# One half of an attention block issued a unit earlier, its scales with it, and some weight conversions and one small transpose issued later

## The chip, the cores and the metric

The kernel runs on one core of one Trainium2 chip. The metric is the device time of one execution in microseconds (us). Five engines work side by side, each through its own list of instructions in a fixed order, and wait for each other through semaphores: PE (TensorE, matrix products into PSUM), DVE (VectorE), ACT (ScalarE), POOL (GpSimd) and SP (SyncE, which here only issues transfers).

## The reference

Attention inside chunks of 64 rows, for 8 batches and 8 heads of 576 rows and 64 columns, and then a feed-forward layer over the 4608 tokens of 512 numbers that this gives:

```python
scores = scale * np.matmul(q_c, k_c.transpose(0, 1, 2, 4, 3))
scores = scores - np.max(scores, axis=-1, keepdims=True)
attn = np.exp(scores)
attn = attn / (np.sum(attn, axis=-1, keepdims=True) + 1e-09)
out = np.matmul(attn, v_c)
...
h = x @ w_in            # 4608 x 512 times 512 x 2048
g = h - np.tanh(h)
return (g @ w_out)      # 4608 x 2048 times 2048 x 512
```

## The kernel before

The tokens are taken in nine groups of 512. Group 0 and group 1 get their attention in a first phase, and their feed-forward layer in full precision (class `FeedForward`). Groups 2 to 8 run with fp16 pairs and a way of multiplying 2x2 blocks with seven products instead of eight (class `Fast`). So two things have to be made ready while group 1 is under way: the fp16 weights, and the attention of group 2. While group g of the seven runs, the attention of group g+1 is made.

**Units.** Group 1 runs in 16 units, called W0 to W15 here (`written`, line 540). A unit makes a first product (line 511, 12 matmuls of 512 columns, into one of two `ph` buffers in PSUM), `shrink` (tanh on ACT at line 518, a subtraction on DVE at line 520, both in place of `ph`), and the second product of an older unit (line 538). What DVE rounds off for the unit before, line 528, ends the use of that unit's `ph`: so the first product of W10 waits for line 528 of W8. Groups 2 to 8 run in 16 units each, F0 to F15 for group 2 (`run`, line 661): a first product (line 590, 24 matmuls), tanh (line 597), `L598` on DVE (the last reader of `ph`), three operations on POOL (lines 599 to 601), and one unit later `split` (line 610 on ACT and 611 on DVE). The second product (line 630, 21 matmuls) uses a unit that is two or three units old. F0 to F3 have no second product of their own, F4 has two, and from F5 each has one.

**What is put between.** The dictionary `at` holds more work by half-units: key 2s is issued behind the first product and `shrink` of unit s, key 2s+1 behind its second product, and keys from 32 on belong to group 2 (32 is F0). An engine meets this work at that place of its list and nowhere else. Three kinds of work lie there:

- the attention of the next group, put by `ahead` (line 695), in two halves b = 0 and 1. First for both: absolute sums of q and k (line 105, ACT), the largest of v (line 288, DVE); `across` turns these sums with a small transpose on PE (line 296) and takes their maximum on DVE (line 298); `spread_out` hands it to all partitions by two tiny matmuls (line 305) and makes the scales `to` (lines 112 to 114, DVE). Then per half: `split` of q, k and v to fp16 pairs with these scales (line 322 on ACT, 323 on DVE), scores (line 333, 96 matmuls on PE), shift (345, 346), exponent (350), totals (355 to 358), division (362), a transpose by DMA (369, 370, 374), and values (333 again, 386, 387). All PSUM work of this kind has one buffer, `psa`.
- `convert` of the first weight matrix (lines 432, 433, 435 and 436), one of 16 in each unit.
- `combine` of the second weight matrix, eight times (lines 450 to 463, POOL), and behind it `shorten` in four parts to fp16 (line 480 on ACT, 481 on DVE). A combination also waits until the one that used its place was shortened.

The order of all engines in this stage is the order in which the program is written (`manual_schedule`).

Of the kernel before, what the change touches and what calls it, by code (L numbers as in the profile page):

```python
# [38 lines left out]
FAST = 2  # L39
# [16 lines left out]
def attn_ffn_kernel(ctx: ExitStack, tc: tile.TileContext, qE, kE, vE, qL, kL, vL, w_in, w_out, out):  # L56
# [41 lines left out]
    def new_half_x():  # L98

        t = xpool.tile([P, KC, MOST], F32R, name="xh").bitcast(F16)  # L100
        return t[:, :, :MOST], t[:, :, MOST:]
# [593 lines left out]
    def ahead(att, at, g):  # L695

        o = 2 * FC * (g - FAST)

        def put(unit, part, f, *args):
            at[o + 2 * unit + part].append(lambda: f(*args))  # L700

        late = g == FAST
        for unit, n in (1, "q"), (2, "k"):
            put(unit, 0, lambda n=n: att.sums(g, n, ffn.tile([P, MOST], F32, name="t", bufs=3)))
        put(1 if g < FAST + 2 else -3, 0, att.halves, g, 0)
        put(1 if late else 2, 1, att.halves, g, 1)
        put(3 if late else 4, 1, att.across, g)
        put(4 if late else 5, 1, att.spread_out, g)
        put(9, 1, lambda: powers.update({g: half.power_of(g)}))
        put(6, 0, lambda: xs.update({g: new_half_x()}))  # L710
        for b, u in enumerate((4, 13) if late else (6, 14)):
            put(u, 1, att.split, g, b, "q")
            put(u + 1, 0, att.split, g, b, "k")
            other = u + 2 if late and b else u + 1
            put(other, 1, att.split, g, b, "v")
            if g + 1 < NG:
                for i in (2 * b, 2 * b + 1):
                    put(u + 1, 1, att.load, FIRST[g + 1] + i, i, "qk")
                    put(other, 1, att.load, FIRST[g + 1] + i, i, "v")
            u += late  # L720
            put(u + 2, 0, att.scores, g, b)
            put(u + 2, 1, att.shifted, g, b)
            put(u + 3, 0, att.exponent, g, b)
            put(u + 3, 1, att.totals, g, b)
            put(u + 4, 0, att.divided, g, b)
            put(u + 5, 0, att.transpose, g, b)
            at[o + 2 * u + 17 - late].insert(0, lambda b=b: att.values(g, b, xs[g]))
# [15 lines left out]
    att = Early(pool, [psum, ps_a], 4)  # L743
# [102 lines left out]
    late = ctx.enter_context(tc.tile_pool(name="att", bufs=1, side="right", reuse_waits="tile"))  # L846
    w_pool.update((fc, late) for fc in SPARE)
    att, half = Late(late), Half(late)
# [4 lines left out]
    xs, powers, at, made = {}, {}, defaultdict(list), {}  # L853
    def make(j, steps):
        if j not in made:
            made[j] = half.combine(j)
        for _ in range(steps):
            next(made[j])
# [11 lines left out]
    for g in range(FAST, NG):  # L870
        ahead(att, at, g)
    for j in range(FC // 2 - 2):
        at[4 * j + 7].append(lambda j=j: make(j, 5 if j else 4))
        if j == 0:
            at[11].append(lambda: make(0, 1))
        for i in range(4):
            at[4 * j + 11 + i].append(lambda j=j, i=i: half.shorten(j, slice(i, i + 1)))
    o = 2 * FC
    for k, j, steps in (o - 1, 6, 5), (o + 1, 7, 2), (o + 3, 7, 1), (o + 5, 7, 1), (o + 7, 7, 1):
        at[k].append(lambda j=j, steps=steps: make(j, steps))  # L880
# [77 lines left out]
```

## Time and profile before

| | |
|---|---|
| median of 3 runs | 812.99 us (812.72 to 813.47) |
| the profiled execution's own time | 813.85 us |
| its span, first to last instruction | 812.0 us |
| mean granted TensorE clock | 1.000 |
| F0 begins on PE at | 217.52 us |
| idle PE before a line-511 product, waiting for line 528 on DVE | 5 times, 4.0 us in all (this counts the weight loads in front of the products) |
| POOL waiting for line 598 | 223.3 us in 102 waits |

All views are of the profiled execution. A row of the timeline has the start in us, the duration in us, the engine, the line, the operation with its output and inputs, the count of merged instructions, and, in brackets, how long the engine had been idle and what ended the wait. A row of the chain has start, share of time on the chain, and what the time went to; durations on the chain leave out what overlaps.

### The profile page before, as it was taken

The page shows a single profiled execution, that of the slowest core. Times are in us where ns is not written, and L with a number is a line of the kernel's source. Part 1 is how long each engine was busy: PE and PEld are TensorE (multiplying, and loading weights), DVE is VectorE, ACT ScalarE, POOL GpSimd, SP SyncE. Part 2 cuts the span into 40 slices and gives each one's busy share as a digit, 9 for nine tenths or more (in the row PEclk, how much of TensorE's full clock was granted, in tenths as well). Part 3 has the DMA queues.
Part 4 walks back from the last instruction along what each step waited for, and adds up shares of the span by engine and source line. Part 5 has one row for each costly group of instructions (what it writes and reads, how often), then busy time and mean ns, then how long its engine had stood idle before and what let it go on. Part 6 is the DMA issues. An engine that isn't in the chain of part 4 may idle for free.

```text
span 812.0 us, 21336 instructions
## 1 busy us (share of the span) xinstructions
PE 798.3 (98%) x9141; PEld 680.7 (84%) x9141; DVE 644.8 (79%) x866; ACT 469.1 (58%) x748; POOL 420.6 (52%) x463
## 2 busy tenths in 40 slices
PE   8999999999999999999999999999999999999997
PEld 4677787777778888888888888888888888888886
DVE  6899997799998968696869687868786878777553
ACT  5698768656776546454745474536454555454332
POOL 1100002296586656574656566565656665656563
PEclk9999999999999999999999999999999999999999
DMA  6954524102221313122222222222222220202000
GB/s 250 343 186 158 170 95 151 63 17 27 66 79 31 96 34 95 38 79 46 80 48 80 53 80 54 79 54 79 53 80 53 80 52 3 54 2 53 2 27 27
DMA packets 59038, 63.23 MB, mean 78 GB/s; under 512 B 32832, under 2 KB 40000, under 8 KB 58944
## 3 DMA queue, kind: packets, MB, share of 16 engines
q1 hardware_dynamic: 58512, 61.23, 25.4%
q8 instruction: 71, 1.16, 0.6%
q10 hardware_dynamic: 432, 0.66, 0.2%
q14 instruction: 23, 0.19, 0.1%
HBM read 45.09 MB, written 9.44 MB: 67 GB/s over the span
## 4 chain that ended last, share of the span: by engine, by line
PE 81%; DVE 9%; ACT 7%; issue 2%; POOL 0%; DVEq 0%; ACTq 0%
PE ph L590 35%; PE po L630 31%; PE ph L511 6%; PE po L538 5%; PE psa L333 3%; PE ph L777 1%; ACT w L131 1%; ACT wh L140 1%; ACT junk L108 1%; ACT s L213 1%; DVE wl L481 1%; DVE gl L528 1%; DVE w L136 1%; ACT gh L527 1%; DVE wl L435 1%
## 5 line engine op out<-in xcount | busy, mean ns | idle before, releaser
L590 PE MATMUL ph<-xh,wl 128*128 128x256 f16 x2520 | 291.3, 273 | 0.3 <-DVE xl L598 0.3
L590 PEld LDWEIGHTS <-wl 128*128 128x128 f16 x2520 | 244.8, 98 | 29.9 <-issue 1.0
L599 POOL TENSOR_TENSOR xl<-xl 128x256 f32<-128x256 f32 x112 | 110.2, 984 | 224.0 <-DVE xl L598 223.3
L597 ACT ACTIVATE t<-ph,sig 128x512 f32<-128x512 f32 x112 | 77.0, 687 | 195.1 <-PE ph L590 193.5
L598 DVE SCALAR_TENSOR_TENSOR xl<-ph,sig,t 128x512 f32<-128x512 f32 x112 | 83.6, 746 | 75.4 <-ACT t L597 75.0
L630 PEld LDWEIGHTS <-wh 128*128 128x128 f16 x1176 | 114.9, 98 | 13.4
L601 POOL TENSOR_TENSOR xl<-xl 128x256 f32<-128x256 f32 x112 | 112.5, 1004 | 0.0
L600 POOL TENSOR_TENSOR xl<-xl 128x128 f32<-128x128 f32 x112 | 107.1, 956 | 0.0
L630 PE MATMUL po<-wl,wh 128*128 128x256 f16 x672 | 104.7, 273 | 0.0
L611 DVE SCALAR_TENSOR_TENSOR gl<-xl,to_g,gh 128x896 f16<-128x896 f32 x56 | 85.4, 1525 | 9.8 <-ACT gh L610 9.6
L630 PE MATMUL po<-wh,wh 128*128 128x256 f16 x504 | 88.6, 273 | 0.0
L611 DVE SCALAR_TENSOR_TENSOR wh<-xl,to_g,wh 128x896 f16<-128x896 f32 x56 | 66.6, 1189 | 27.4 <-ACT wh L610 27.4
L610 ACT ACTIVATE wh<-xl,to_g 128x896 f16<-128x896 f32 x56 | 58.2, 1039 | 49.5 <-POOL xl L601 49.5
L630 PEld LDWEIGHTS <-gh 128*128 128x128 f16 x784 | 75.7, 98 | 9.2
L630 PE MATMUL po<-wh,gh 128*128 128x256 f16 x392 | 63.5, 273 | 0.0
L630 PE MATMUL po<-wl,gh 128*128 128x256 f16 x392 | 61.1, 273 | 0.0
L610 ACT ACTIVATE gh<-xl,to_g 128x896 f16<-128x896 f32 x56 | 57.8, 1032 | 1.2 <-POOL xl L601 1.2
L538 PE MATMUL po<-wh,gh 128*128 128x512 f32 x128 | 52.1, 407 | 0.9 <-ACT gh L527 0.5
L538 PE MATMUL po<-wl,gh 128*128 128x512 f32 x128 | 50.7, 396 | 0.9 <-POOL wl L144 0.9
L410 POOL PARTITION_ALL_REDUCE top<-most x2 | 0.7, 371 | 97.7 <-DVE most L408 97.7
L630 PEld LDWEIGHTS <-gl 128*128 128x128 f16 x392 | 38.3, 98 | 4.5
L630 PE MATMUL po<-wh,gl 128*128 128x256 f16 x196 | 40.5, 273 | 0.0
(147 smaller groups left out, 1352.9 us busy)
## 6 DMA issues: line engine op xcount, KB each, us to landing
raw<-w_in SPq DMA_DIRECT2D x16, 512.0 KB, 3.6
raw<-w_out SPq DMA_DIRECT2D x16, 512.0 KB, 4.5
rawk<-kL SPq DMA_DIRECT2D x28, 256.0 KB, 3.3
rawv<-vL SPq DMA_DIRECT2D x28, 256.0 KB, 3.6
xl<-qL SPq DMA_DIRECT2D x28, 256.0 KB, 3.2
out<-wh SPq DMA_DIRECT2D x55, 128.0 KB, 1.8
q<-qE SPq DMA_DIRECT2D x8, 256.0 KB, 5.4
v<-vE SPq DMA_DIRECT2D x8, 256.0 KB, 5.0
```

Of the source, the lines that this page charges most:

```text
L333: nc.tensor.matmul(ps(c, e, hp)[u * D:(u + 1) * D], lhsT=stationary(a, r, e, hp, u), rhs=moving(b, r, e, hp, u), start=(i == 0), stop=(i = ...
L511: nc.tensor.matmul(ph, lhsT=wt[fc][0][a][:, kc * P:(kc + 1) * P], rhs=x[b][:, kc, cols], start=(k == 0), stop=(k == 3 * KC - 1))
L538: nc.tensor.matmul(self.po[t], lhsT=gg[a][:, ts], rhs=wt[fc][1][b], start=(fc == 0 and a == b), stop=(fc == FC - 1 and a == 1))
L590: nc.tensor.matmul(self.ph[:, 1 - f::2, :], lhsT=half_w[fc][:, w, kc * P:(kc + 1) * P], rhs=rhs, start=(k == 0), stop=(k == 3 * KC - 1))
L597: nc.scalar.activation(t, self.ph, AF.Tanh, scale=sig)
L598: nc.vector.scalar_tensor_tensor(out=u[:, :4], in0=self.ph, scalar=sig, in1=t, op0=ALU.mult, op1=ALU.subtract)
L599: nc.gpsimd.tensor_add(u[:, 4:6], u[:, 1:3], u[:, 0:4:3])
L600: nc.gpsimd.tensor_add(u[:, 6], u[:, 1], u[:, 2])
L601: nc.gpsimd.tensor_sub(u[:, 0:4:3], u[:, 0:2], u[:, 2:4])
L610: nc.scalar.activation(gh, u, AF.Copy, scale=powers[1])
L611: nc.vector.scalar_tensor_tensor(out=gl, in0=u, scalar=powers[1], in1=gh, op0=ALU.mult, op1=ALU.subtract)
L630: nc.tensor.matmul(place[m], lhsT=part[:, self.SUM[m]], rhs=w[m][:, o], start=first, stop=(last and part is gl), skip_group_check=True)
```

## The change

```diff
@@ ahead(): the attention of group g, issued while the group before runs
-        put(3 if late else 4, 1, att.across, g)
-        put(4 if late else 5, 1, att.spread_out, g)
+        later = g == FAST + 1
+        put(2 if late else 4 + later, not later, att.across, g)
+        put(3 if late else 5, not late, att.spread_out, g)
         put(9, 1, lambda: powers.update({g: half.power_of(g)}))
         put(6, 0, lambda: xs.update({g: new_half_x()}))
-        for b, u in enumerate((4, 13) if late else (6, 14)):
+        for b, u in enumerate((3, 13) if late else (6, 14)):
@@ conversions of the combined weights
         for i in range(4):
-            at[4 * j + 11 + i].append(lambda j=j, i=i: half.shorten(j, slice(i, i + 1)))
+            at[4 * j + 11 + i + (2 if j > 3 and i else 0)].append(lambda j=j, i=i: half.shorten(j, slice(i, i + 1)))
```

`late` is true for group 2 alone, whose attention runs under W0 to W15. Its `across` moves from behind the second product of W3 to behind that of W2, its `spread_out` from behind the second product of W4 to behind the first product of W3, and every step of its half 0 moves one unit ahead, with the loads of the next group that follow it. For group 3 (the fourth) `across` moves from behind the second products of F4 to behind the first product of F5; its `spread_out` stays behind the second product of F5. For the combinations j = 4 and 5 (the fifth and sixth), the parts 1 to 3 of `shorten` move one unit back. No instruction is added or taken out.

Three places show it. The first is DVE's list around F3 to F6. The names: `xl<-ph` (line 598) belongs to F4 and F5 in turn, line 611 to F3 and F4, line 298 is the maximum in `across` of group 3, and lines 112 to 114 are its `spread_out`. Before:

```order
L481 SCALAR_TENSOR_TENSOR wh_2619<-wl_2611,to_w,wh_2619 128x512
L598 SCALAR_TENSOR_TENSOR xl<-ph,sig,t 128x512
L611 SCALAR_TENSOR_TENSOR wh_2633<-xl,to_g,wh_2632 128x896
L481 SCALAR_TENSOR_TENSOR wl_2620<-wh_2612,to_w,wl_2620 128x512
L298 TENSOR_REDUCE most<-psa 3x1
L598 SCALAR_TENSOR_TENSOR xl<-ph,sig,t 128x512
L611 SCALAR_TENSOR_TENSOR gl<-xl,to_g,gh 128x896
L481 SCALAR_TENSOR_TENSOR wh_2621<-wh_2608,to_w,wh_2621 128x256
L112 TENSOR_SCALAR from<-psa 128x3
```

The same place of the changed kernel (buffer numbers differ by two):

```order
L481 SCALAR_TENSOR_TENSOR wh_2617<-wl_2609,to_w,wh_2617 128x512
L598 SCALAR_TENSOR_TENSOR xl<-ph,sig,t 128x512
L611 SCALAR_TENSOR_TENSOR wh_2631<-xl,to_g,wh_2630 128x896
L481 SCALAR_TENSOR_TENSOR wl_2618<-wh_2610,to_w,wl_2618 128x512
L598 SCALAR_TENSOR_TENSOR xl<-ph,sig,t 128x512
L611 SCALAR_TENSOR_TENSOR gl<-xl,to_g,gh 128x896
L298 TENSOR_REDUCE most<-psa 3x1
L481 SCALAR_TENSOR_TENSOR wh_2619<-wh_2606,to_w,wh_2619 128x256
L112 TENSOR_SCALAR from<-psa 128x3
```

Line 298 now stands behind line 598 of F5 and line 611 of F4; on PE, line 305 still stands behind the second product of F5, and the first product of F6 behind line 305.

The second place is ACT's list from F1 to F2. Line 480 is `shorten`, line 562 writes out group 1's result, the two rows of line 597 are tanh of F1 and F2. Before:

```order
L597 ACTIVATE t<-ph,sig 128x512
L610 ACTIVATE gh<-xl,to_g 128x896
L350 ACTIVATE psa<-psa,exp 128x1024
L105 ACTIVATE t,sums<-xl 128x2048
L480 ACTIVATE wh_2306<-wh_2497,to_w 128x256
L562 COPY wh_2626<-po_1602 128x512
L562 COPY wh_2627<-po_1603 128x512
L562 COPY wh_2628<-po_1604 128x512
L562 COPY wh_2629<-po_1605 128x512
L597 ACTIVATE t<-ph,sig 128x512
L610 ACTIVATE gh<-xl,to_g 128x896
```

The same place of the changed kernel:

```order
L597 ACTIVATE t<-ph,sig 128x512
L610 ACTIVATE gh<-xl,to_g 128x896
L350 ACTIVATE psa<-psa,exp 128x1024
L105 ACTIVATE t,sums<-xl 128x2048
L480 ACTIVATE wh_2508<-wl_2500,to_w 128x512
L562 COPY wh_2624<-po_1602 128x512
L562 COPY wh_2625<-po_1603 128x512
L562 COPY wh_2626<-po_1604 128x512
L562 COPY wh_2627<-po_1605 128x512
L480 ACTIVATE wl_2509<-wh_2501,to_w 128x512
L597 ACTIVATE t<-ph,sig 128x512
L610 ACTIVATE gh<-xl,to_g 128x896
```

Between tanh of F1 and tanh of F2 stand now two conversions of 512 columns instead of one of 256. DVE's list has the same two (line 481) ahead of line 598 of F2, and the one of 256 columns behind line 362 in F2. In exchange two conversions of 512 columns went from ahead of line 528 of W14 to behind it.

The third place is PE's list around the small transpose of group 2 (line 296). Before, behind the second product of W3:

```order
L538 MATMUL po_1604<-wh_1083,gl 128x512
L538 MATMUL po_1605<-wh_1083,gl 128x512
L296 MATMUL psa<-ident,sums 3x128
L511 MATMUL ph<-xh,wh_78 128x512 x4
L511 MATMUL ph<-xh,wl_79 128x512 x4
L511 MATMUL ph<-xl,wh_78 128x512 x4
```

In the changed kernel, behind the second product of W2:

```order
L538 MATMUL po_1604<-wh_72,gl 128x512
L538 MATMUL po_1605<-wh_72,gl 128x512
L296 MATMUL psa<-ident,sums 3x128
L511 MATMUL ph<-xh,wh_1085 128x512 x4
L511 MATMUL ph<-xh,wl_1086 128x512 x4
L511 MATMUL ph<-xl,wh_1085 128x512 x4
L305 MATMUL psa<-ident,most 128x3
```

Line 296 moved ahead of W3's first and second product. Line 305, which stood behind the second product of W4, moved ahead of that one, of W4's first product and of W3's second.

## The prediction

> **What bounds the kernel now.** I read the page first: busy shares and the shares of the chain.
>
> ```profile
> PE 798.3 (98%) x9141; PEld 680.7 (84%) x9141; DVE 644.8 (79%) x866; ACT 469.1 (58%) x748; POOL 420.6 (52%) x463
> ...
> PE 81%; DVE 9%; ACT 7%; issue 2%; POOL 0%; DVEq 0%; ACTq 0%
> ```
>
> PE bounds it, and the change takes no matmul away. So time can only come from, or go into, PE's waits. The second view is PE's timeline from 140 us on, reduced to the rows that show idle time in brackets (W10, W11, W12, F0, F4, then line 296 of group 3 behind F4).
>
> ```profile
> 180.98 1.20 PE L511 MATMUL ph<-xh,wh 128*128 128x512 f32 x4 [1.01 <-DVE gl L528]
> ...
> 187.38 1.19 PE L511 MATMUL ph<-xh,wh 128*128 128x512 f32 x4 [0.53 <-DVE gl L528]
> ...
> 193.30 1.20 PE L511 MATMUL ph<-xh,wh 128*128 128x512 f32 x4 [0.20 <-DVE gl L528]
> ...
> 217.52 1.47 PE L590 MATMUL ph<-xh,first_place 128*128 128x256 f16 x12 [0.65 <-DVE gl L528]
> ...
> 235.12 2.78 PE L590 MATMUL ph<-xh,wl 128*128 128x256 f16 x24 [0.30 <-DVE xl L598]
> ...
> 243.34 0.27 PE L296 MATMUL psa<-ident,sums 128*3 128x128 f32 x1 [0.85 <-DVE a L370]
> ```
>
> Together 3.54 us, all of them waits for DVE, and all in the stretch that the change touches. Behind it PE has next to no waits; a window of one group of seven (PE busy is the second number) shows it:
>
> ```profile
> 262.66:346.00 83.34, 83.31 (x1103) 73.91 (x1102) 66.44 (x84) 45.06 (x57) 50.61 (x55) 1.00 0.25 65
> ```
>
> So whatever shift PE has at about 250 us arrives at the end unchanged. I work out that shift.
>
> **The change part by part.**
>
> *Line 296 of group 2, now behind W2.* It needs the sum of k from ACT. The rows: ACT's last part of that sum, and the chain around W3.
>
> ```profile
> 140.05 0.21 ACT L105 ACTIVATION_READ_ACCUMULATOR t<-rawk 128x1 f32 x1
> ...
> 139.26 3.00 PE ph L511 x12
> ...
> 144.98 0.11 PE psa L296
> 145.09 2.79 PE ph L511 x12
> ...
> 150.99 2.96 PE ph L511 x12
> ```
>
> PE reaches the new place at about 139.26, the sum is there at 140.26. Line 296 then starts at 140.30 and takes 0.27 (as it did after its wait at 243.34), so W3's first product starts at 140.57, not 139.26: 1.31 late. It no longer pays the start after a wait (3.00 against 2.79, 0.21), and the 0.11 of line 296 is gone from behind W3. Cost: 1.31 - 0.21 - 0.11 = **+1.0 us**. Line 305 behind W3's first product finds its maximum ready, since a whole first product lies between and the step on DVE is short; it costs nothing new.
>
> *Scales and half 0 earlier: what DVE gains.* DVE waited for this before, then had its three `split` steps and the conversions in one run without idle time:
>
> ```profile
> 144.43 0.69 DVE L520 TENSOR_TENSOR ph<-ph,t 128x512 f32<-128x512 f32 x1
> ...
> 151.03 0.16 DVE L112 TENSOR_SCALAR from<-psa 128x3 f32<-128x3 f32 x1 [1.78 <-PE psa L305]
> ...
> 152.81 1.28 DVE L323 SCALAR_TENSOR_TENSOR wh<-xl,to,wh 128x1024 f16<-128x1024 f32 x1 [1.17 <-ACT wh L322]
> ...
> 158.73 0.74 DVE L481 SCALAR_TENSOR_TENSOR wl<-wh,to_w,wl 128x512 f16<-128x512 f32 x1
> ...
> 180.25 0.68 DVE L528 TENSOR_TENSOR gl<-ph,gh 128x512 fp32r<-128x512 f32 x1
> ...
> 183.56 1.22 DVE L362 TENSOR_TENSOR psa<-psa,sm 128x1024 f32<-128x1024 f32 x1
> ...
> 214.50 1.22 DVE L481 SCALAR_TENSOR_TENSOR wh<-wl,to_w,wh 128x512 f16<-128x512 f32 x1
> ```
>
> DVE reaches the scales behind line 520 of W3 (144.43), near 145.1 instead of 151.03, and the three steps of 1.28 fill idle places. The first conversion (158.73) then only waits for PE: W5's first product ends at 153.95 + 1.0, tanh and line 520 take some 0.6 each, so it comes near 156.2, 2.5 earlier. POOL's next combination waits for that conversion and starts 2.5 earlier too; a conversion takes 1.22 while POOL works and 0.74 when it doesn't. Not all of this lead lasts: in W6 DVE must wait for PE's tanh, and line 362 (1.22) now stands ahead of line 528 of W8. That line ended at 180.93; plus 1.2, less 0.6 to 1.1 for two or three steps in the gaps that POOL leaves, it ends between 181.0 and 181.5. PE would be at W10 at 180.98 - 1.01 + 1.0 = 180.97: a wait of at most 0.6, not 1.01. For W11 POOL is through earlier than before, and little of the 0.53 stays. For W12 line 370 is gone from ahead of it, which is longer than its 0.20: no wait. The bounds are no gain, and all three waits with three starts of 0.2, 2.3 us; I take **-1.3 us**, a little above the middle, since two of three waits lose their cause.
>
> *Conversions later, first end.* Two DVE conversions leave the place ahead of line 528 of W14, for which F0 waits 0.65. One of them took 1.22 (214.50); the gap closes even though lines 387 and W12's work now come earlier. With the start after a wait **-0.8 us**.
>
> PE's shift at F1 is so +1.0 - 1.3 - 0.8 = **-1.1 us**; by the bounds +1.0 to -2.1.
>
> *Conversions later, second end, and line 296 of group 3.* This part decides. From the end of F1's first product, ACT, DVE and POOL hand one chain to each other without a gap:
>
> ```profile
> 224.18 2.65 PE ph L590 x24
> ...
> 231.26 0.50 ACT L480 ACTIVATE wh<-wh,to_w 128x256 f16<-128x256 f32 x1
> ...
> 235.25 1.58 DVE L611 SCALAR_TENSOR_TENSOR gl<-xl,to_g,gh 128x896 f16<-128x896 f32 x1 [0.18 <-ACT gh L610]
> ...
> 244.30 0.74 DVE L598 SCALAR_TENSOR_TENSOR xl<-ph,sig,t 128x512 f32<-128x512 f32 x1
> ...
> 245.12 1.56 POOL L599 TENSOR_TENSOR xl<-xl 128x256 f32<-128x256 f32 x1 [0.15 <-DVE xl L598]
> ...
> 248.26 1.04 ACT L610 ACTIVATE gh<-xl,to_g 128x896 f16<-128x896 f32 x1 [1.24 <-POOL xl L601]
> ...
> 249.34 1.62 DVE L611 SCALAR_TENSOR_TENSOR gl<-xl,to_g,gh 128x896 f16<-128x896 f32 x1 [1.25 <-ACT gh L610]
> 250.89 0.47 DVE L481 SCALAR_TENSOR_TENSOR wh<-wh,to_w,wh 128x256 f16<-128x256 f32 x1
> ```
>
> The last three steps are F4's: line 598 at 244.30, POOL until line 610 can start, line 610, line 611. Nothing on PE waited for this end of the chain before, since line 298 stood ahead of it. Now line 298 is queued behind this line 611, and line 305 on PE waits for line 298:
>
> ```profile
> 247.16 0.27 DVE L298 TENSOR_REDUCE most<-psa 3x1 f32<-3x128 f32 x1
> ...
> 248.53 0.31 PE psa L305 x2
> 248.84 2.74 PE ph L590 x24
> ```
>
> With the chain as before, line 298 would start at 250.89, end at 251.16, line 305 start at 251.20 and, with 0.17 for the start after a wait, F6's first product at 251.68. It started at 248.84: **+2.84 us**. The moved conversions lengthen the chain. On ACT, ahead of tanh of F2, one of 512 columns stands for one of 256, and one more is added; the first costs 0.22 and the second 0.62 to the next start (a 512 takes 0.71 against 0.50 here):
>
> ```profile
> 220.93 0.71 ACT L480 ACTIVATE wh<-wl,to_w 128x512 f16<-128x512 f32 x1
> ...
> 231.80 0.57 DVE L481 SCALAR_TENSOR_TENSOR wh<-wh,to_w,wh 128x256 f16<-128x256 f32 x1 [0.96 <-ACT wh L480]
> ...
> 206.70 0.90 DVE L481 SCALAR_TENSOR_TENSOR wh<-wh,to_w,wh 128x256 f16<-128x256 f32 x1
> ```
>
> On DVE the 256 one comes in behind line 362, 0.5 to 1.0 (0.57 or 0.90 here). Together 1.3 to 1.9; **+1.6 us**, nearer the slow row, since POOL is busy there. The 0.85 that line 296 waits, and the 0.30 at F4 (which grows to some 1.4, line 598 of F2 being later), change nothing in this: PE waits at line 305 for the chain anyhow. PE's work from F1's first product to line 305 is about 21.7 us, the chain 24.3 + 1.6, so the wait there should be near 4.2 us.
>
> **Sum:** -1.1 + 2.84 + 1.6 = **+3.3 us**. It is made against the profiled execution (span 812.0, its own time 813.85, 0.9 above the median); a shift is the same for both, so I add it to the median: 812.99 + 3.3 = **816.3 us**. About 0.2%, 1.6 us, is what a measurement of this kernel can tell from no change.
>
> **Rivals.**
>
> *The early relief does not come.* DVE's lead is lost in W6 and POOL contention stays: the -1.3 is 0, and the sum +4.6, 817.6 us. For it: no row of DVE between its line 323 for k and line 435 of W12 has a wait in brackets. Against: two costly steps leave W10 and W11.
>
> *The wait slows the matmuls behind it.* The trace's first 15 warming matmuls took 6.17 us, 0.41 each, and the later 20 took 0.22 each:
>
> ```profile
> 1.17 6.17 PE L777 MATMUL ph<-warm 128*128 128x512 bf16 x15 [1.17 <-DVE warm L740]
> ...
> 8.36 4.49 PE L777 MATMUL ph<-warm 128*128 128x512 bf16 x20
> ```
>
> So PE runs at about half speed after standing still long enough, and a wait of 4.2 us is four times the longest of before. If it happened once for as long, it would cost 15 x 0.19 = 2.8 us: 819.1 us. Against: the profile gives 1.00 as the granted clock everywhere, and after 1.01 us idle the products ran as fast as ever. [...] No run so far shows where the limit lies.
>
> *The chain is shorter than worked out.* Two fast rows:
>
> ```profile
> 248.20 0.72 POOL L599 TENSOR_TENSOR xl<-xl 128x256 f32<-128x256 f32 x1
> ...
> 228.51 1.20 DVE L611 SCALAR_TENSOR_TENSOR gl<-xl,to_g,gh 128x896 f16<-128x896 f32 x1 [0.18 <-ACT gh L610]
> ```
>
> Where POOL and DVE do not slow each other (line 599 at 0.72 instead of 1.56, line 611 at 1.20 instead of 1.62), it loses 1.3, and if all of W10 to W12 is gained too, the sum is 2.84 + 1.3 - 1.3 - 2.1 = +0.7: 813.7 us.
>
> *Covered after all, and faster.* If line 298 ended before F5's second product does, line 305 would not wait, and PE would keep -1.1, lose the 0.85 at line 296 with its start (-1.0) and pay 1.1 more at F4: -1.0, or -2.0 with all of W10 to W12; I put it at 811.2 us. The point from which this decides is a chain of under 21.7 us from F1's first product, where the rows give 24.3 without anything added. That the change doesn't do what it says is excluded by the order.
>
> **How the numbers follow.** Forecast 0.58; no relief 0.12; half speed 0.12; shorter chain 0.12; covered 0.06. The range 813.6 to 818.2 leaves out half speed and covered, 0.18. Slower by over 0.2% are the first three, 0.82; within 0.2% the shorter chain, 0.12; faster the last, 0.06.
>
> **What would show it.** In the changed profile: line 305 at about 251 to 253 us with PE idle for about 4 us ahead of it, waiting for DVE's line 298, itself straight behind a line 611; line 296 of group 3 without a wait; line 296 of group 2 with 1.0 us; F0 without a wait; F4 with over 1 us; W10 to W12 with under 0.7 in all. It would be wrong if the wait at line 305 is under 2 us, or if other waits appear behind 255 us.

## The result, and the profile after

The changed kernel takes 817.51 us (median of 4 runs, 816.83 to 818.36), the kernel before 812.86: a ratio of 1.0057, 95% interval 1.0039 to 1.0074, 4.65 us slower. The prediction was 816.3 us with a range of 813.6 to 818.2.

The profiled execution took 817.97 us, its span is 816.2 us, against 812.0 before. These are the rows of PE's timeline of the changed kernel with idle time in brackets, from 137 to 300 us, and the row behind the last of them:

```profile
140.03 0.27 PE L296 MATMUL psa<-ident,sums 128*3 128x128 f32 x1 [1.11 <-ACT t L105]
...
233.96 2.78 PE L590 MATMUL ph<-xh,wl 128*128 128x256 f16 x24 [1.70 <-DVE xl L598]
...
250.22 0.58 PE L305 MATMUL psa<-ident,most 3*128 3x3 f32 x2 [3.87 <-DVE most L298]
250.74 5.04 PE L590 MATMUL ph<-xh,wl 128*128 128x256 f16 x24
```

The waits at W10, W11, W12, F0 and at line 296 of group 3 are gone. Three are left: the new one of 1.11 us at line 296 of group 2, the one at F4, grown from 0.30 to 1.70, and 3.87 us at line 305. And one thing is no wait: F6's first product takes 5.04 us in this row, where the same 24 matmuls took 2.79 before. DVE's timeline shows what line 305 waited for:

```profile
243.98 1.13 DVE L611 SCALAR_TENSOR_TENSOR wh<-xl,to_g,wh 128x896 f16<-128x896 f32 x1
245.04 1.21 DVE L481 SCALAR_TENSOR_TENSOR wl<-wh,to_w,wl 128x512 f16<-128x512 f32 x1
246.18 0.74 DVE L598 SCALAR_TENSOR_TENSOR xl<-ph,sig,t 128x512 f32<-128x512 f32 x1
248.36 1.62 DVE L611 SCALAR_TENSOR_TENSOR gl<-xl,to_g,gh 128x896 f16<-128x896 f32 x1 [1.44 <-ACT gh L610]
249.90 0.27 DVE L298 TENSOR_REDUCE most<-psa 3x1 f32<-3x128 f32 x1
250.09 0.46 DVE L481 SCALAR_TENSOR_TENSOR wh<-wh,to_w,wh 128x256 f16<-128x256 f32 x1
```

Line 298 took 0.27 us and could have run at 245: its input, the output of line 296, was there at 244.06. But it stood in the list behind line 611 of F4, and that one waited another 1.44 us for ACT. Windows of the changed kernel say what became of the clock (the number ahead of the last two is the granted TensorE clock; the windows are PE's wait, F6's first product and what follows it):

```profile
246.31:250.18 3.87, 0.04 (x1) 0.00 (x0) 2.43 (x4) 2.05 (x3) 2.71 (x5) 0.79 0.00 0
250.74:255.71 4.97, 4.97 (x26) 3.39 (x26) 1.21 (x5) 0.00 (x0) 0.00 (x0) 0.53 0.00 0
255.71:258.92 3.21, 3.21 (x119) 2.93 (x119) 2.15 (x2) 2.10 (x3) 1.50 (x2) 1.00 0.02 5
```

The clock fell during the wait and came back only at the end of F6's first product. In steps of 0.25 us the same trace has two values and two steps between them: 1.00 up to 248.50, then 0.61, 0.50 in every step from 248.75 to 255.25, then 0.74, and 1.00 from 255.50. So 0.79 over 3.87 us is 1.6 us at half speed, and the clock fell about 2.2 us into the wait; 0.53 over 4.97 us leaves 0.3 us at full speed at the end. That makes one stretch of some 6.8 us at half speed. The chain of the changed kernel closes the account:

```profile
221.61 2.65 PE ph L590 x24
...
250.22 0.58 PE psa L305 x2
250.80 4.98 PE ph L590 x24
```

F1's first product ends at 224.26 instead of 226.83 (-2.57, of which 0.28 comes from a first phase that ended earlier: W2 starts at 133.06 instead of 133.34). F6's starts at 250.80 instead of 248.84 (+1.96), and takes 4.98 instead of 2.74 (+2.24). The last two make +4.20, the difference of the spans to within 0.1 us; behind it the shift stays.

### The profile page after: what moved, and what is told of

Same layout as the page of the kernel before. It is cut to its first block, busy times and chain, and to the rows that moved or that the text cites. A ratio compares the mean times of both kernels' runs of the same rounds, so it can differ in the third digit from the quotient of the medians.

```text
span 816.2 us, 21334 instructions
## 1 busy us (share of the span) xinstructions
PE 799.0 (98%) x9139; PEld 682.2 (84%) x9141; DVE 644.7 (79%) x866; ACT 469.1 (57%) x748; POOL 422.0 (52%) x463
## 4 chain that ended last, share of the span: by engine, by line
PE 87%; ACT 7%; DVE 4%; issue 1%; POOL 1%; DVEq 0%; ACTq 0%
PE ph L590 35%; PE po L630 31%; PE ph L511 8%; PE po L538 7%; PE psa L333 3%; PE ph L778 1%; ACT wh L140 1%; ACT junk L108 1%; ACT s L213 1%; ACT w L131 1%; ACT t L105 1%; DVE w L136 1%; ACT t L518 1%; ACT gh L527 1%; DVE w L137 1%
```

## The experiments

The wait theory: the loss is the wait at line 305 and the slow clock behind it, the early part of the change is a gain. Most of the kernels below say in their expectation what another theory would make of them. In the kernels with added matmuls, lines 305 and 590 are numbered 309 and 594.

**Across of group 3 put back.**

```diff
-        later = g == FAST + 1
+        later = False
```

> The changed kernel, but with across of group 3 back behind the second products of F4. Wait theory (the loss is the 3.9 us that line 305 waits for line 298, and the slow matmuls behind it): that wait is gone, the granted clock is 1.000, F4 still waits 1.7 us, line 296 waits about 1.0 us for line 370, and F5 starts about 1 us earlier than in the kernel before: 811.8 us, between 811.0 and 812.5. Rival (the moved conversions and the earlier half are what costs, and the wait at line 305 would only turn up elsewhere): slower than before by 1 us or more, with a new long wait behind F5.

Measured: 812.79 us (11 runs, 812.43 to 813.21) against 812.78; ratio 0.9999, interval 0.9991 to 1.0008. PE's timeline from F4 on:

```profile
234.27 2.78 PE L590 MATMUL ph<-xh,wl 128*128 128x256 f16 x24 [1.70 <-DVE xl L598]
...
242.66 0.27 PE L296 MATMUL psa<-ident,sums 128*3 128x128 f32 x1 [1.03 <-DVE a L370]
...
247.77 0.38 PE L305 MATMUL psa<-ident,most 3*128 3x3 f32 x2
248.08 2.79 PE L590 MATMUL ph<-xh,wl 128*128 128x256 f16 x24
```

The waits are the expected ones, line 305 waits for nothing, and F6's first product is back at 2.79. The whole loss of the change hangs on this one edit. But the time is 1.0 above what I expected, and outside the expected range: the rest of the change gains nothing in sum. The next run shows why.

**Across of group 3 alone.** The changed line of `across` for group 3, everything else as before.

```diff
-        put(3 if late else 4, 1, att.across, g)
+        later = g == FAST + 1
+        put(3 if late else 4 + later, not later, att.across, g)
```

> The kernel before, with across of group 3 alone moved behind the first product of F5. Wait theory: line 305 starts at about 251.2 us as in the prediction's term of 2.84, PE waits about 3.6 us for it, and F6's first product starts 2.8 us late; 815.7 us where the clock holds, up to 818 where the first product of F6 runs at half speed as in the changed kernel. Rival: within 0.5 us of the kernel before, since only the other two edits cost.

Measured: 817.13 us (5 runs, 816.85 to 817.36), ratio 1.0051, interval 1.0039 to 1.0064: 4.35 us slower. PE's timeline:

```profile
179.99 1.20 PE L511 MATMUL ph<-xh,wh 128*128 128x512 f32 x4 [0.35 <-DVE gl L528]
...
234.04 2.78 PE L590 MATMUL ph<-xh,wl 128*128 128x256 f16 x24 [0.30 <-DVE xl L598]
...
250.13 0.38 PE L305 MATMUL psa<-ident,most 3*128 3x3 f32 x2 [3.70 <-DVE most L298]
250.44 4.21 PE L590 MATMUL ph<-xh,wl 128*128 128x256 f16 x24
```

The wait is 3.70 where 3.6 was expected. From F4 to F6's first product it takes 16.40 us against 13.65 before (235.12 to 248.77): +2.75, the prediction's term of 2.84. The rest of the 4.35 us is 1.6, and the slow clock accounts for it: F6's first product takes 4.21 in place of 2.79, and two windows show the clock granted meanwhile:

```profile
248.00:252.00 4.00, 1.87 (x15) 1.64 (x16) 3.42 (x8) 1.24 (x3) 0.93 (x2) 0.95 0.00 0
252.00:256.00 4.00, 4.00 (x113) 2.85 (x112) 0.53 (x1) 1.25 (x2) 0.00 (x0) 0.62 0.00 0
```

Worked out as above, with the two values of the changed kernel, that is 0.4 and 3.0 us at half speed. Taken as one stretch, it was 3.4 us long, half of that of the changed kernel, and began about 1.5 us after the wait had ended; this is an estimate from the two windows.

The first row of the timeline teaches something else. Up to F4 this kernel runs the list of the kernel before, yet W10 waits 0.35, not 1.01. (The run of the conversions alone, further down, has the same list up to W12 and waits 0.41.) A row of DVE's timeline of this kernel, in W8:

```profile
172.53 0.73 DVE L435 SCALAR_TENSOR_TENSOR wl<-wh,to_w,wl 128x512 f16<-128x512 f32 x1
```

and the same instruction in the kernel before:

```profile
172.91 1.32 DVE L435 SCALAR_TENSOR_TENSOR wl<-wh,to_w,wl 128x512 f16<-128x512 f32 x1
```

POOL was at work in both, between other instructions of its own, so the prediction's 1.22 us for a conversion while POOL works and 0.74 when it doesn't do not hold for every row; why the times differ stays open. From the start of W2's first product to the end of F1's, this kernel took 92.76 us (132.98 to 225.74), the profiled execution of before 93.49. So that execution spent 0.73 us there that this one did not: its waits, from which I took the possible gain, were on the high side.

That also settles the run with `across` put back. It took 91.20 us for the same stretch, 1.56 less than 92.76; it then lost 1.40 at F4 and 0.18 at line 296 of group 3, and nothing is left.

**PE kept busy during the wait.** The changed kernel, with matmuls between the second product of F5 and line 305:

```diff
             top = d["ps"][:, P:P + 3]
+            if g == FAST + 1:
+                idle = ps_h.tile([P, MOST], F32, name="ph")
+                for _ in range(17):
+                    nc.tensor.matmul(idle, lhsT=half_w[0][:, 0, :P], rhs=half_w[0][:, 0, :], start=True, stop=True)
```

> The changed kernel with 17 added matmuls of 128x512 fp16 (about 3.7 us, result unused) on PE between the second product of F5 and line 305, so that PE works while it would wait. Theory of the idle clock: F6's first product takes 2.6 to 2.8 us instead of 5.0, the granted clock is 1.000, line 305 starts when it did: 2.2 us less than the changed kernel, about 815.3 us. Rival (the slow product has another cause, such as line 333 or the load of the chip at that place): it stays at 5.0 us and the time at 817.5.

Measured: 815.32 us (7 runs, 815.06 to 815.47), ratio 1.0030, interval 1.0019 to 1.0041. PE's timeline:

```profile
246.01 3.83 PE L308 MATMUL ph<-first_place 128*128 128x512 f16 x17
250.05 0.38 PE L309 MATMUL psa<-ident,most 3*128 3x3 f32 x2 [0.20 <-DVE most L298]
250.36 2.79 PE L594 MATMUL ph<-xh,wl 128*128 128x256 f16 x24
```

More work for PE makes the kernel 2.2 us faster than the changed one. Line 305 starts when it did, and F6's first product has its 2.79 again. The window from 250.10 to 258.00 us has a granted clock of 1.00, where the same window of the changed kernel has 0.67. That settles the clock: it was the idle time, not the place.

**Shorter waits, to find the limit.** The same with 8 matmuls.

```diff
-                for _ in range(17):
+                for _ in range(8):
```

> The same with 8 added matmuls (about 1.8 us), so that PE still waits about 2.1 us at line 305. Theory of the idle clock with a limit above 2.1 us: clock 1.000 and F6's first product at 2.6 to 2.9 us, 815.3 us. With a limit below 2.1 us: half speed again, 817.5 us. Line 305 starts when it did in the changed kernel in both cases.

Measured: 816.07 us (5 runs, 815.20 to 816.55). PE's timeline:

```profile
246.74 1.89 PE L308 MATMUL ph<-first_place 128*128 128x512 f16 x8
250.77 0.38 PE L309 MATMUL psa<-ident,most 3*128 3x3 f32 x2 [2.14 <-DVE most L298]
251.08 2.79 PE L594 MATMUL ph<-xh,wl 128*128 128x256 f16 x24
```

In the profiled execution nothing was lost behind 2.14 us of idling: F6's first product has its 2.79, and the granted clock from 250.10 to 258.00 us is 1.00. The execution is longer than that with 17 matmuls because its first phase ran later (line 296 of group 2 at 140.56 against 139.85). Whether one of the other four executions lost something stays open; the slowest, at 816.55, has a mean granted clock of 0.997, where those with 17 matmuls have 0.998 to 1.000. With 4 and with 2 matmuls:

```diff
-                for _ in range(17):
+                for _ in range(4):
...
-                for _ in range(17):
+                for _ in range(2):
```

> The changed kernel with 4 added matmuls ahead of line 305, so that PE waits there about 3.0 us. Theory of the idle clock: the limit lies between 2.1 us (no loss seen) and 3.7 us (half speed). Half speed again, F6's first product over 4 us and about 817 us, if the limit is under 3.0; 2.7 us and 815.3 us if it is above.

> The same with 2 added matmuls: PE waits about 3.4 us. [...]

Measured with 4: 816.7 us (4 runs: 815.31, 816.61, 816.79, 816.88); with 2: 817.65 us (4 runs, 816.78 to 818.62). PE's timeline with 4, then with 2:

```profile
246.01 1.03 PE L308 MATMUL ph<-first_place 128*128 128x512 f16 x4
250.04 0.38 PE L309 MATMUL psa<-ident,most 3*128 3x3 f32 x2 [3.00 <-DVE most L298]
250.35 4.28 PE L594 MATMUL ph<-xh,wl 128*128 128x256 f16 x24
```

```profile
250.03 0.38 PE L309 MATMUL psa<-ident,most 3*128 3x3 f32 x2 [3.44 <-DVE most L298]
250.35 4.46 PE L594 MATMUL ph<-xh,wl 128*128 128x256 f16 x24
```

3.00 us without matmuls were enough for half speed in the profiled execution. By their times two of the three others lost it too and one, at 815.31, did not, so it differed from execution to execution. Windows of the two runs, again with 4 and then with 2 matmuls:

```profile
248.00:252.00 4.00, 1.96 (x15) 1.71 (x16) 3.42 (x8) 1.15 (x3) 0.84 (x2) 0.93 0.00 0
252.00:256.00 4.00, 4.00 (x113) 2.90 (x112) 0.56 (x1) 1.28 (x2) 0.00 (x0) 0.64 0.00 0
```

```profile
248.00:252.00 4.00, 1.97 (x12) 1.50 (x13) 3.43 (x8) 1.14 (x3) 0.83 (x2) 0.83 0.00 0
252.00:256.00 4.00, 4.00 (x116) 3.04 (x115) 0.38 (x1) 1.10 (x2) 0.00 (x0) 0.74 0.00 0
```

Worked out in the same way, both had a stretch of some 3.4 us at half speed, and it began about 1.4 and 0.6 us after line 309 had started. So in these runs the slow clock set in when the wait was already over: with 4 matmuls, with 2 and with `across` alone the granted clock is 1.00 from 246.30 to 250.10 us and 0.78 from 250.10 to 258.00.

**The conversions alone.**

```diff
-            at[4 * j + 11 + i].append(...)
+            at[4 * j + 11 + i + (2 if j > 3 and i else 0)].append(...)
```

> The kernel before with the conversions of the fifth and sixth combination moved, nothing else. Wait theory: W10 to W12 wait as before, F0 does not wait (0.5 to 0.65 less), F4 waits 1.7 us instead of 0.3 (F4's first product starts 9.7 us after the end of F1's instead of 8.3), line 296 waits about 1 us as before; net about +0.9: 813.7 us. Rival (the conversions are the whole early gain): faster by over 1 us.

Measured: 813.72 us (11 runs, 813.35 to 814.16) against 812.82, ratio 1.0011, interval 1.0002 to 1.0020. All the rows of PE's timeline from 118 to 330 us with a wait:

```profile
180.37 1.21 PE L511 MATMUL ph<-xh,wh 128*128 128x512 f32 x4 [0.41 <-DVE gl L528]
...
186.76 1.20 PE L511 MATMUL ph<-xh,wh 128*128 128x512 f32 x4 [0.52 <-DVE gl L528]
...
192.69 1.20 PE L511 MATMUL ph<-xh,wh 128*128 128x512 f32 x4 [0.18 <-DVE gl L528]
...
235.15 2.78 PE L590 MATMUL ph<-xh,wl 128*128 128x256 f16 x24 [1.70 <-DVE xl L598]
...
243.54 0.27 PE L296 MATMUL psa<-ident,sums 128*3 128x128 f32 x1 [1.03 <-DVE a L370]
```

They free F0 and cost 1.4 at F4, a loss of 0.9 as expected. By the order of the lists the two conversions between tanh of F1 and of F2 delay line 598 of F2, which F4's first product needs; the last run below tests that.

**The earlier half alone.**

```diff
-        put(3 if late else 4, 1, att.across, g)
-        put(4 if late else 5, 1, att.spread_out, g)
+        put(2 if late else 4, 1, att.across, g)
+        put(3 if late else 5, not late, att.spread_out, g)
...
-        for b, u in enumerate((4, 13) if late else (6, 14)):
+        for b, u in enumerate((3, 13) if late else (6, 14)):
```

> The kernel before with half 0 of group 2's attention, its scales and its small transpose one unit earlier, nothing else. Wait theory: line 296 of group 2 waits 1.1 us, no wait at W10 to W12, the wait at F0 stays at 0.5 us or more because DVE reaches line 528 of W14 late, F4 and line 296 of group 3 as before; net -0.3 to -1.0: 812.1 us. Rival (the earlier half costs what it gains): within 0.2 us of the kernel before.

Measured: 811.53 us (11 runs, 811.14 to 812.22), ratio 0.9984, interval 0.9975 to 0.9992: 1.3 us faster, more than expected. All the rows of PE's timeline from 118 to 330 us with a wait:

```profile
139.82 0.27 PE L296 MATMUL psa<-ident,sums 128*3 128x128 f32 x1 [1.10 <-ACT t L105]
...
232.45 2.78 PE L590 MATMUL ph<-xh,wl 128*128 128x256 f16 x24 [0.41 <-DVE xl L598]
...
240.67 0.27 PE L296 MATMUL psa<-ident,sums 128*3 128x128 f32 x1 [0.86 <-DVE a L370]
```

The wait at F0 is gone without the conversions. I had expected it to stay. From W2's start to the end of F1's first product this kernel takes 91.18 us, the changed one 91.20: the conversions add nothing there once the half is earlier.

**The half, and the conversions of the fifth combination only.** As the last one, and

```diff
-            at[4 * j + 11 + i].append(...)
+            at[4 * j + 11 + i + (2 if j == 4 and i else 0)].append(...)
```

> Half 0 earlier, and the conversions of the fifth combination alone one unit later; those of the sixth and across of group 3 as in the kernel before. Wait theory: no wait at W10 to W12 and at F0 as in the changed kernel (F1's first product ends 1.5 us earlier than in the kernel before), and F4 waits 0.3 to 0.7 instead of 1.7, since the two conversions ahead of tanh of F2 are gone again; line 296 waits 0.9: 811.4 us, between 811.0 and 812.0. Rival (DVE has no room left at W15, so F0 or F2 waits instead): 812.5 or more.

Measured: 811.36 us (11 runs, 811.03 to 811.56), ratio 0.9982, interval 0.9973 to 0.9991: 1.5 us faster than the kernel before. PE waits in three places:

```profile
140.03 0.27 PE L296 MATMUL psa<-ident,sums 128*3 128x128 f32 x1 [1.09 <-ACT t L105]
...
232.69 2.78 PE L590 MATMUL ph<-xh,wl 128*128 128x256 f16 x24 [0.43 <-DVE xl L598]
...
240.90 0.27 PE L296 MATMUL psa<-ident,sums 128*3 128x128 f32 x1 [0.85 <-DVE a L370]
```

It beats both kernels. Against the half alone (811.53) the difference is inside the spread of the runs. It differs from the run with `across` put back (812.79) only in the conversions of the sixth combination, which stay where they were: F4 waits 0.43 instead of 1.70. So those are the ones that cost 1.4 us.

## Why the prediction came out as it did

The direction, the place and the mechanism of the wait were right: line 298 behind line 611 of F4, line 305 behind line 298, everything on PE behind line 305. The edits measured alone give +4.35 for `across`, +0.90 for the conversions and -1.29 for the half, 3.96 in all; the change gives 4.65. The clock can account for the 0.7 between: F6's first product lost 1.4 in the profile of `across` alone and 2.2 in that of the change. That the gain at F0 is in two edits but can be had once belongs there too; no run separates the two. Step by step:

- **Line 296 of group 2, +1.0.** Right. Expected: start at 140.30, W3's first product 1.31 late. Measured: a wait of 1.11, and W3's first product 7.24 us behind W2's start (133.06 to 140.30) where it was 5.92 (133.34 to 139.26): 1.32 late.
- **W10 to W12, -1.3, and F0, -0.8.** The sum of the early part was under-sized: forecast -1.1 with the +1.0, measured -2.29 against the profiled execution of before (91.20 against 93.49), -1.56 against the run with the same list (92.76). All the waits vanished, not most. The attribution of F0 was too narrow: I gave it to the conversions, and either edit alone frees it, the earlier half as well as the conversions.
- **The chain from F1 to line 298, 24.3 + 1.6 us.** Right: from the end of F1's first product (224.26) to the end of line 298 (250.18 on the chain) it is 25.92. With `across` alone, where the conversions stay, it is 24.35, so they added 1.57. The wait was to be near 4.2 and was 3.87, since F4's wait ahead of it came to 1.70, not some 1.4.
- **The clock.** This is the step that failed. I set "The wait slows the matmuls behind it" beside the forecast as a rival with 0.12, when it was the forecast's own consequence: it came on top of the wait. It cost 2.24 in the profiled execution and 2.2 by the medians (817.51 against 815.32 with PE kept busy). The 0.12 was my own estimate: no row of before shows how long PE must stand still for it, and the warming matmuls are no measure of it, since the granted clock is 1.00 from 1.00 to 7.50 us, where 15 of them took 0.41 us each. Here 3.00 us without matmuls were followed by half speed in the profiled execution, and 2.14 us were not. The four executions of the changed kernel fall into two pairs: 816.83 and 817.05 with a mean granted clock of 0.997, 817.97 and 818.36 with 0.995. The profiled one, with its 6.8 us at half speed, is of the slower pair; 3.4 us at half speed would fit the faster pair, but no trace shows it.

Without the clock the change would be 815.32 - 812.78 = +2.5 us, not +3.3: most of that difference is the early part, forecast too small by some 0.5. The missing clock, 2.2, pulled the other way and was larger. That the time lies inside the range is partly luck: the lack of early relief, and not the clock, had carried the range up to 818.2.

## What to carry to other kernels

When a small step is moved to spare PE a wait, look at what stands ahead of it in the list of the next engine: 0.27 us of DVE work, queued behind an instruction that itself waits for two engines, became 3.9 us on PE, over four times the wait that it removed. In this kernel profiled waits of PE of 3.00 to 3.87 us also made the matmuls behind them slower, 1.42 to 2.25 us more for F6's first product, so such a wait is to be priced with both; 17 matmuls whose result nobody uses, put into the wait, brought the second part back (2.79 us for F6's first product). And waits of a single profiled execution should be compared with a second one before a gain is read from them: 0.7 of the 2.4 us at W10 to F0 were not there in the next execution of the same list.

## What the runs showed of the hardware

- In the profiled executions, after 3.00 us without matmuls (4 added), 3.44 (2 added), 3.70 (`across` alone) and 3.87 (the change), F6's first product took 4.28, 4.46, 4.21 and 5.04 us in place of 2.79; after 2.14 (8 added) and 0.20 us (17 added) it took 2.79. With 3.00 us one of four executions seems to have been spared, by its time of 815.31 us. In the window of the slow product of the changed kernel the granted clock was 0.53, in steps of 0.25 us 0.50 until 255.25.
- The stretch at half speed, an estimate from the windows, was some 3.4 us long behind the waits of 3.00, 3.44 and 3.70 us and some 6.8 us with that of 3.87. It began 0.6 to 1.5 us after the end of the wait in the first three and about 2.2 us into the wait in the last.
- The same DVE instruction (line 435 in W8), with the same list on all engines up to there, took 0.73 us in one execution (`across` alone) and 1.32 in another (the kernel before), with POOL at work in both. The cause stays open.
